# A retention and cosine-gated layer on Trainium2: S, Y and A as quarters of one block with swapped key halves, loads behind the preceding slot's transposes, the first k ahead of the iotas

## The chip, the core and the metric

The kernel runs on one core of one Trainium2 chip. The metric is the device time of one execution in microseconds; 8 runs of the kernel before have a median of 210.26 (210.06 to 210.48). One further execution was taken with the profiler.

## The reference

Two layers follow each other. The first is a retention recurrence with a fixed decay per head; the second is a two-matrix layer gated with a cosine.

```python
B, H, S, D = 4, 8, 768, 64
gamma = 1.0 - 2.0 ** (-5.0 - np.arange(H))
for t in range(S):
    state = gamma * state + k[t] (outer) v[t]        # per batch and head, 64 x 64
    y[t] = D ** -0.5 * q[t] @ state
x = y.transpose(0, 2, 1, 3).reshape(B * S, H * D)    # 3072 x 512
h = x @ w_in                                         # 512 x 2048
out = (h * np.cos(h)) @ w_out                        # 2048 x 512
```

## The kernel before

**Slots.** The sequence is cut into 6 chunks of 128 tokens. A slot `p` is one chunk of two batches (b = 0, 1), 12 slots in all; `ORDER` starts with chunk 0 of both batch pairs and goes through the rest one pair after the other. Within a chunk the recurrence is written as matrix products:

- q and k are loaded (`load`), scaled and cast to bf16 (`conv_q`, `conv_k`; `conv_v` scales v by a decay `gk` that depends on the token's place), and turned so that the head dimension lies in the partitions: by TensorE with `t_mm` and `t_copy` for slots 0 to 5, by a transposing DMA (`dma_t`, on SP) from slot 6 on.
- **A** (`a_mm`): the scores of the chunk's 128 keys against its 128 queries, for 16 pairs of batch and head. DVE multiplies them by a causal mask (`a_mask`, into `am`).
- **Y**: the output of the slot. The first part ("inter", line 428) takes the old state `stb` times q; the second (`intra`, line 414) takes the masked scores times v.
- **S** (`s_mm`, line 460): the state gains k times v, in the PSUM bank `st_ps`; `s_copy` casts it to `stb` for the next slot.

**Quarters.** A and Y work on matrices with 64 rows and 64 columns of weights, and so use the 128x128 array as four quarters: (row half, column half), by `tile_position`. S used two column strips of 128 rows. Where two row halves add into the same PSUM bank, they take turns: `y1_mm` gives one half of the keys to each batch, `hop` is an empty instruction on another engine (SP for slots up to 5, POOL after that) that waits for the end of this first part, and `y2_mm`, which exchanges the halves, waits for it. `intra` leaves out queries 0 to 63 where keys are 64 to 127, since the mask is zero there (64 columns instead of 128); A computed them.

**The block of a slot** in steady state is inter, first part of Y, hop, A of the next slot, second part of Y, S. Around it run the wide matmuls: `f_mm` (x times w_in, four of 512 columns), cosine on ACT (`f_cos`), product on DVE (`f_mul`), and `o_mm` (times w_out), evacuated by ACT (`o_out`) and stored through SP (`o_dma`). Groups of four chunks go through 16 steps `s`, each one `f_mm` of group g and one quarter of an `o_mm` of group g-1; the block of a slot follows step 3 and step 11. The last output tile is split in two halves of 256 columns (`last_o`).

**Order.** Each engine runs its instructions in the order in which they were issued. Up to slot 5 a planner (`Plan`) orders the work with costs, due ranks (`RF`, `RM`, a random addition of `JIT` with seed `SEED`), and counts of free PSUM banks and DMA semaphores; `LOADS` is the order of the loads that POOL issues, `HALF0` says how many of group 0's w_in columns are done slot by slot (`h_mm`). Where the plan has nothing for TensorE early on, `idle_mm` fills with zero matmuls. Past the plan, a hand-written loop issues `block`, `conv` and loads of later slots on SP.

**The start.** POOL makes three iotas, then issues the loads of k, q and k of the slots 0 and 1 (names "K", "Q1", "K1") and v; SP issues the two halves of slot 0's q. DVE makes `dist`, the identity and the mask from the iotas, ACT eight decays `dec` from `dist`, then `gq` and `gk`. Slots 0 and 1 differ: A is a full 128-row product (`a_mm` with `p < 2`), masked with `dec`; one of its tiles is saved by ACT (`a_save`) and masked by POOL (`a_late`) for each slot; `y_first` is the slot's Y, with v as it was loaded (`raw_v`).

Of the kernel before, what the change touches and what calls it, by code (L numbers as in the profile page):

```python
# [162 lines left out]
SEED, JIT, HOLD = 60, 4.0, "PD"  # L163
HALF0, SPARE, RF, RM, COLD = 4, 1, 40.0, 40.0, 5.2
# [3 lines left out]
def kernel(  # L168
# [24 lines left out]
    ORDER = [0, NC] + [x for x in range(1, NP) if x != NC]  # L193
    LATE = NC
# [39 lines left out]
    mask = sb([128, 128], BF16, "mask")  # L234
# [3 lines left out]
    gk = sb([128, NC, H], FP32, "gk")  # L238
# [27 lines left out]
    def load(eng, p, names):  # L266

        bp, c = divmod(ORDER[p], NC)
        for n in names.split():
            t, src = SRC[n[0].lower()]  # L270
            if len(n) == 1:
# [4 lines left out]
                        "b h t d -> t (b h) d"))  # L276
            else:
# [33 lines left out]
    def conv_v(p, b, e):  # L311
        ENG[e].tensor_tensor(out=vb(p)[:, b], in0=vf[p % PRE][:, b],  # L312
                             in1=bc(gk, ORDER[p] % NC), op=ALU.mult)

# [38 lines left out]

    def a_mm(p, u):
        n = p % NB
        bk = held["a", p, u] = [banks.take(), banks.take()]
        ap = [t.rearrange("p (a t) -> p a t", a=HP) for t in bk]
        for a in range(HP):
            h = 4 * u + a
            for x in range(1 if p < 2 else 2):  # L360
                for b in range(2):
                    if p < 2:
                        nc.tensor.matmul(ap[b][:, a, :], lhsT=kt(n, b, h), rhs=qt(n, b, h),
                                         tile_position=(64 * b, 0))
                        continue
                    nc.tensor.matmul(ap[b][ts(x, 64), a, :], lhsT=kt(n, b, h)[:, ts(x, 64)],  # L366
                                     rhs=qt(n, b, h), tile_position=(64 * b, 64 * x),
                                     skip_group_check=True)

    def a_mask(p, b, u):  # L370
        bank = held["a", p, u][b]
        nc.vector.tensor_tensor(  # L372
            out=am[p % 2][b][u], in0=bank.rearrange("p (a t) -> p a t", a=HP),
            in1=(dec[:, b] if p < 2 else mask.unsqueeze(1).to_broadcast([128, HP, 128])),
            op=ALU.mult)
        banks.give(bank)
# [32 lines left out]
    def intra(p, b, a, x, **kw):  # L409

        ms = []
        for j in range(2):
            h = 2 * a + j
            ms.append(nc.tensor.matmul(  # L414
                held["yp", p][b][ts(j, 64), a, 64 * x :], lhsT=vs[p % NB][ts(x, 64), b, h, :],
                rhs=am[p % 2][b][h // 4][ts(x, 64), h % 4, 64 * x :],
                start=False, stop=True, tile_position=(64 * x, 64 * j), skip_group_check=True))
        return ms

    def y1_mm(p):  # L420
# [3 lines left out]
        for a in range(HP):  # L424
            for b in range(2):
                for j in range(2):
                    h = 2 * a + j
                    nc.tensor.matmul(  # L428
                        held["yp", p][b][ts(j, 64), a, :], lhsT=stb[p % 2][ts(b, 64), h, :],
                        rhs=qt(p % NB, b, h), start=(a == 0), stop=False,  # L430
                        tile_position=(64 * b, 64 * j), skip_group_check=True)
        for a in range(HP):
            held["part", p] = intra(p, 1, a, 1) + intra(p, 0, a, 0)

    def hop(p):
        ms = held["part", p]
        held["hop", p] = (nc.sync if p <= 5 else nc.gpsimd).nop(nofuse=True)
        for m in ms:
            after(m, held["hop", p])

    def y2_mm(p):
        for a in range(HP):
            for m in intra(p, 1, a, 0) + intra(p, 0, a, 1):
                if a == 0:
                    after(held["hop", p], m)
# [6 lines left out]

    def has_s(p):
        return p != 1 and (p == LATE or ORDER[p] % NC < NC - 1)

# [75 lines left out]
    def last_o(g, j):  # L531

        o = ob[o_no[0] % 4]
        for hf in range(2):
            bank = banks.take()
            for f in range(KOUT):
                nc.tensor.matmul(bank[:, :256], lhsT=gt[g % 2][:, f, ts(j, 128)],  # L537
                                 rhs=w_out_sb[:, f, ts(hf, 256)],
                                 start=(f == 0), stop=(f == KOUT - 1))
            copy("AD"[hf], o[:, ts(hf, 256)], bank[:, :256])  # L540
            (nc.sync, nc.scalar)[hf].dma_start(
                out=out[ds(o_row(g, j), C), ts(hf, 256)], in_=o[:, ts(hf, 256)])
# [8 lines left out]

    nc.gpsimd.iota(pos, pattern=[[C, NC]], base=1, channel_multiplier=1,
# [5 lines left out]
    load(nc.sync, 0, "q0 q1")  # L558
    load(nc.gpsimd, 0, "K")
# [9 lines left out]
    nc.vector.tensor_scalar(out=mask, in0=dist, scalar1=0.0, scalar2=None, op0=ALU.is_ge)  # L569
# [10 lines left out]
    nc.scalar.activation(out=gk, in_=lgp, func=AF.Exp, scale=-1.0)  # L580
    nc.scalar.activation(out=lnsc, in_=halfpi, func=AF.Sin)
# [9 lines left out]
    HM, HCQ, HCV = "q2", "", ""  # L591
    plan = Plan({"bank": 7, "cos": 3, "sem": 8, "out": 4, "port": 1, "ring": 7}, 6.5)
# [7 lines left out]
    ld["q", 0, 0], ld["q", 0, 1], ld["k", 0, 0], ld["k", 0, 1] = map(at, (3.9, 5.0, 7.4, 7.4))  # L600
# [287 lines left out]
```

## Time and profile before

| what | value |
|---|---|
| median of 8 runs | 210.26 us (210.06 to 210.48) |
| the profiled execution, its own time | 210.43 us |
| its span in the profile | 208.6 us |
| TensorE busy | 201.7 us (97%) |
| ScalarE, VectorE, GpSimd busy | 115.9, 108.0, 80.0 us |
| granted TensorE clock, mean | 0.998 |
| data moved by DMA | 32.05 MB |

PE is TensorE, PEld its weight loads, DVE VectorE, ACT ScalarE, POOL GpSimd, SP SyncE, which only issues DMAs and carries waits here. Times in rows count from the span's start. Matmuls are pipelined: a row's extent holds the tail of its last matmul too, so distances between starts say more than extents. "[0.27 <-POOLq ...]" behind a row is idle time of that engine and what ended it. Some matmul records can be missing, so a count of 14 may stand beside a row of 2.

### The profile page before, as it was taken

The numbers are of one execution on the slowest core, as the hardware profiler recorded it, in microseconds if no ns is written. First come the engines' busy times: TensorE is split into PE (matmuls) and PEld (weight loads), VectorE is DVE, ScalarE is ACT, GpSimd is POOL, SyncE is SP. The second block draws the span as 40 slices with busy tenths as digits, with TensorE's granted clock in tenths as the row PEclk, the third lists the DMA queues.
The fourth block names the chain that finished last, engine by engine and source line by source line (L and its number), as shares of the span: only waits on it lengthen the run. The fifth ranks groups of instructions, "written<-read, shape, count | busy, mean of one in ns | idle before, by whom it ended". The sixth has DMA issues, their size and how long they took to land.

```text
span 208.6 us, 4799 instructions
## 1 busy us (share of the span) xinstructions
PE 201.7 (97%) x1994; PEld 109.2 (52%) x2017; DVE 108.0 (52%) x186; ACT 115.9 (56%) x194; POOL 80.0 (38%) x84
## 2 busy tenths in 40 slices
PE   7999999999999999999999999999999999999993
PEld 2547456789555545445455455454444444444462
DVE  5474888977725647438438438338332334443000
ACT  7677788579655456556556556554545553553120
POOL 8789979999999007007007007000000000000000
PEclk9999999999999999999999999999999999999999
DMA  7999999999999599999894602401101101110222
GB/s 123 185 258 225 309 250 291 209 335 343 343 293 182 148 232 245 229 216 247 201 256 29 176 0 54 150 0 57 50 0 53 50 9 44 50 50 21 80 79 76
DMA packets 57495, 32.05 MB, mean 154 GB/s; under 512 B 46592, under 2 KB 51968, under 8 KB 57472
## 3 DMA queue, kind: packets, MB, share of 16 engines
q0 software_dynamic: 14352, 15.47, 33.6%
q1 hardware_dynamic: 42976, 16.13, 31.8%
q8 instruction: 16, 0.26, 0.5%
q10 hardware_dynamic: 144, 0.13, 0.2%
q14 instruction: 7, 0.06, 0.1%
HBM read 27.26 MB, written 6.29 MB: 161 GB/s over the span
## 4 chain that ended last, share of the span: by engine, by line
PE 91%; DMA 3%; POOL 2%; issue 1%; DVE 1%; POOLq 0%; DVEq 0%
PE bank L517 38%; PE bank L472 31%; PE bank L493 8%; DMA vf<-in_v_dram 3%; PE bank L366 3%; PE bank L414 2%; PE st_ps L460 2%; PE bank L337 2%; PE bank L537 2%; PE bank L428 2%; PE bank L546 1%; POOL ks L273 1%; PE bank L395 1%; POOL qs L273 1%; POOL kx L273 1%
## 5 line engine op out<-in xcount | busy, mean ns | idle before, releaser
L480 ACT ACTIVATE cosb<-bank,halfpi 128x512 bf16<-128x512 f32 x96 | 65.5, 689 | 57.4 <-PE bank L472 46.4
L517 PE MATMUL bank<-w_out_sb,gt 128*128 128x512 bf16 x360 | 90.1, 379 | 0.9 <-issue 0.3
L484 DVE TENSOR_TENSOR gt<-bank,cosb 128x512 bf16<-128x512 f32 x76 | 51.6, 688 | 55.3 <-ACT cosb L480 55.3
L472 PE MATMUL bank<-xt,w_in_sb 128*128 128x512 bf16 x289 | 74.8, 379 | 0.8 <-issue 0.3
L517 PEld LDWEIGHTS <-gt 128*128 128x128 bf16 x368 | 35.7, 98 | 42.3
L472 PEld LDWEIGHTS <-w_in_sb 128*128 128x128 bf16 x304 | 28.9, 98 | 34.0 <-DMA w_in_sb<-in_moe_w_in_dram 0.2
L308 POOL TENSOR_TENSOR qs<-qf,gq 128x512 bf16<-128x512 f32 x18 | 18.5, 1044 | 44.9 <-PE bank L414 44.8
L372 DVE TENSOR_TENSOR am<-bank,mask 128x512 bf16<-128x512 f32 x40 | 24.8, 679 | 0.3 <-PE bank L366 0.3
L312 POOL TENSOR_TENSOR vs<-vf,gk 128x512 bf16<-128x512 f32 x22 | 22.7, 1044 | 1.5 <-DMA vf<-in_v_dram 1.2
L297 ACT COPY ob<-bank 128x512 f32<-128x512 f32 (+1 forms) x24 | 13.8, 576 | 15.5 <-PE bank L517 13.9
L493 PE MATMUL bank<-xt,w_in_sb 128*128 128x256 bf16 x160 | 18.8, 273 | 0.0
L297 ACT CAST xt<-bank 128x512 bf16<-128x512 f32 x24 | 12.9, 589 | 9.7 <-PE bank L414 9.0
L501 DVE TENSOR_TENSOR gt<-bank,cosb 128x512 bf16<-128x512 f32 x20 | 13.5, 688 | 8.8 <-ACT cosb L480 8.8
L493 PEld LDWEIGHTS <-w_in_sb 128*128 128x128 bf16 x160 | 15.4, 98 | 2.7
L299 DVE CAST stb<-st_ps 128x512 bf16<-128x512 f32 x10 | 6.9, 689 | 11.1 <-PE st_ps L460 11.1
L546 PE MATMUL bank<-zero 128*128 128x512 bf16 x33 | 10.8, 455 | 1.1 <-DVE halfpi L562 1.1
L297 ACT CAST ks<-kf 128x512 bf16<-128x512 f32 x20 | 11.5, 629 | 0.0
L273 POOL DMA_DIRECT2D vf<-in_v_dram x8 | 9.5, 1194 | 0.0
L297 ACT COPY qkt<-bank 128x512 bf16<-128x512 bf16 x13 | 7.1, 594 | 2.8 <-PE bank L337 2.5
L414 PE MATMUL bank<-am,vs 64*64 64x64 bf16 (+1 forms) x320 | 8.3, 205 | 0.1
L299 DVE COPY ob<-bank 128x256 f32<-128x256 f32 x1 | 0.4, 425 | 13.4 <-PE bank L537 13.4
L366 PE MATMUL bank<-qkt 64*64 64x128 bf16 x320 | 7.2, 218 | 0.0
(59 smaller groups left out, 109.7 us busy)
## 6 DMA issues: line engine op xcount, KB each, us to landing
out_dram<-ob SPq DMA_DIRECT2D x23, 256.0 KB, 2.3
vf<-in_v_dram POOLq DMA_DIRECT2D x8, 512.0 KB, 8.5
qf<-in_q_dram POOLq DMA_DIRECT2D x6, 512.0 KB, 10.3
kf<-in_k_dram POOLq DMA_DIRECT2D x6, 512.0 KB, 9.8
w_out_sb<-in_moe_w_out_dram POOLq DMA_DIRECT2D x4, 512.0 KB, 12.5
qf<-in_q_dram SPq DMA_DIRECT2D x4, 512.0 KB, 4.4
kf<-in_k_dram SPq DMA_DIRECT2D x4, 512.0 KB, 6.2
vf<-in_v_dram SPq DMA_DIRECT2D x4, 512.0 KB, 6.6
```

Of the source, the lines that this page charges most:

```text
L273: eng.dma_start(out=t.rearrange("p b h d -> p (b h) d"), in_=src[ds(2 * bp, 2), :, ds(c * C, C), :].rearrange("b h t d -> t (b h) d"))
L297: nc.scalar.copy(out=out, in_=in_)
L308: ENG[e].tensor_tensor(out=qb(p)[:, b], in0=qf[p % PRE][:, b], in1=bc(gq, ORDER[p] % NC), op=ALU.mult)
L312: ENG[e].tensor_tensor(out=vb(p)[:, b], in0=vf[p % PRE][:, b], in1=bc(gk, ORDER[p] % NC), op=ALU.mult)
L366: nc.tensor.matmul(ap[b][ts(x, 64), a, :], lhsT=kt(n, b, h)[:, ts(x, 64)], rhs=qt(n, b, h), tile_position=(64 * b, 64 * x), skip_group_che ...
L372: nc.vector.tensor_tensor(out=am[p % 2][b][u], in0=bank.rearrange("p (a t) -> p a t", a=HP), in1=(dec[:, b] if p < 2 else mask.unsqueeze(1 ...
L472: nc.tensor.matmul(bank, lhsT=w_in_sb[:, i, ts(f, 128)], rhs=xt[g % 2][:, i, :], start=(i == 0), stop=(i == KIN - 1))
L480: nc.scalar.activation(out=cb, in_=bank, func=AF.Sin, bias=halfpi)
L484: nc.vector.tensor_tensor(out=gt[g % 2][:, f, :], in0=bank, in1=cb, op=ALU.mult)
L493: nc.tensor.matmul(bank[:, ts(e, 256)], lhsT=w_in_sb[:, i, ts(f + e, 128)], rhs=xt[g % 2][:, i, ts(hf, 256)], start=(i == 0 and e == 0), s ...
L501: nc.vector.tensor_tensor(out=gt[g % 2][:, f : f + 2, ts(hf, 256)], in0=bank.rearrange("p (f t) -> p f t", f=2), in1=cb.rearrange("p (f t) ...
L517: nc.tensor.matmul(bank, lhsT=gt[g % 2][:, f, ts(j, 128)], rhs=w_out_sb[:, f, :], start=(f == 0), stop=(f == KOUT - 1))
```

## The change

- **One block in quarters** (`y_block`). S is split into two row halves of 64 keys, so that it too uses quarters: 32 matmuls instead of 16, in two parts with a hop between them. Inter, Y, S and the A of the next slot are listed per row half and put in an order by `quarters`, which always takes the matmul whose quarter is free first; second parts are held back for 250 ns after the first by its reckoning. Hops go to SP for slots up to 4, to POOL after that.
- **A leaves out its dead quarter**: 64 columns where keys are all later than the queries. From slot 8 on (`SWAP`) the two halves of the keys are exchanged for half of the heads, by loads in pieces ("ks", "vs": six DMAs each), so that the dead quarter falls on different row and column halves. There are a second mask and a table `gk3` with exchanged halves, filled by three small DMAs on SP.
- **Loads past the plan**: slot p+3 instead of p+4, issued behind the transposes of p+2; v's behind the next output store. The output store of a step now stands ahead of the transposes.
- **Start**: k of slot 0 is issued before the iotas; the second half of slot 0's q on ACT's queue.
- **End**: the last output tile is split 384 and 128.
- **Plan**: no random addition, `HALF0` 6 instead of 4, other due ranks, a few loads in another place, other costs for the blocks.

```diff
-SEED, JIT, HOLD = 60, 4.0, "PD"
-HALF0, SPARE, RF, RM, COLD = 4, 1, 40.0, 40.0, 5.2
+SEED, JIT, HOLD = 0, 0.0, "PD"
+HALF0, SPARE, RF, RM, COLD = 6, 1, 50.0, 30.0, 5.2
...
+            elif n[1] == "s":
+                fl = t[p % PRE].rearrange("p b h d -> p (b h) d")
+                for x in range(2):
+                    for lo, n4, th in ((0, 4, x), (4, 8, 1 - x), (12, 4, x)):
+                        eng.dma_start(
+                            out=fl[ts(x, 64), ds(lo, n4), :],
+                            in_=src[ds(2 * bp, 2), :, ds(c * C + 64 * th, 64), :]
+                            .rearrange("b h t d -> t (b h) d")[:, ds(lo, n4), :])
...
+    def second(p, x, b, u):
+        return x ^ (u ^ b if p >= SWAP else 0)
+    def a_one(p, ap, u, a, b, x):
+        h, lo = 4 * u + a, 64 * second(p, x, b, u)
+        return nc.tensor.matmul(
+            ap[b][ts(x, 64), a, lo:], lhsT=kt(p % NB, b, h)[:, ts(x, 64)],
+            rhs=qt(p % NB, b, h)[:, lo:], tile_position=(64 * b, 64 * x), skip_group_check=True)
...
+    def quarters(rows):
+        free = [[0.0, 0.0], [0.0, 0.0]]
+        left = [list(r) for r in rows]
+        while left[0] or left[1]:
+            best = None
+            for r in range(2):
+                for c in range(2):
+                    nxt = next((m for m in left[r] if m[0] == c), None)
+                    if nxt:
+                        t = max(free[r][c], nxt[2])
+                        if best is None or t < best[0]:
+                            best = (t, r, nxt)
+            t, r, m = best
+            left[r].remove(m)
+            free[r][m[0]] = t + m[1] / 2.4
+            m[3]()
+    def hop_on(p):
+        return nc.sync if p <= 4 else nc.gpsimd
...
+    def s_part(p, r):
+        x = 1 if p == LATE else p
...
+                    m = nc.tensor.matmul(
+                        st_ps[ts(b, 64), h, :], lhsT=kb(x)[ts(r, 64), b, h, :],
+                        rhs=vb(x)[ts(r, 64), b, h, :],
+                        start=(ORDER[x] % NC == 0 and h == 0 and r == 0), stop=True,
+                        tile_position=(64 * r, 64 * b), skip_group_check=True)
...
+    def told(what, p, part, m):
+        key = (what, p)
+        if part == 0:
+            held.setdefault(("ms", key), []).append(m)
+            if len(held["ms", key]) == (32 if what == "y" else 16):
+                w = held["hop", key] = hop_on(p).nop(nofuse=True)
+                for x in held.pop(("ms", key)):
+                    after(x, w)
+        elif held.get(("first", key), 0) < 4:
+            held["first", key] = held.get(("first", key), 0) + 1
+            after(held["hop", key], m)
...
+    def y_block(p, a_next):
...
+        t1 = sum(m[1] for m in y_inter(p, 0) + y_part(p, 0, 0)) / 4.8 + 250
+        t2 = sum(m[1] for m in y_inter(p, 0) + y_part(p, 0, 0) + s_part(p, 0)) / 4.8 + 250
+        for r in range(2):
+            ms = y_inter(p, r) + y_part(p, r, 0)
+            if has_s(p) and r == 0:
+                ms += s_part(p, 0)
+            if a_next:
+                ms += a_rows(p + 1, r)
+            ms += late(y_part(p, r, 1), t1)
+            if has_s(p) and r == 1:
+                ms += late(s_part(p, 1), t2)
+            rows.append(ms)
+        return quarters(rows)
...
-        for hf in range(2):
+        for i, (lo, n) in enumerate(((0, 384), (384, 128))):
...
+    load(nc.gpsimd, 0, "K")
+    load(nc.sync, 0, "q0")
+    load(nc.scalar, 0, "q1")
     nc.gpsimd.iota(pos, pattern=[[C, NC]], base=1, channel_multiplier=1,
...
-    load(nc.sync, 0, "q0 q1")
-    load(nc.gpsimd, 0, "K")
...
+    for x in range(2):
+        nc.vector.tensor_scalar(out=mask[1][ts(x, 64), :], in0=dist[ts(x, 64), :],
+                                scalar1=(64.0, -64.0)[x], scalar2=None, op0=ALU.is_ge)
...
+    for x in range(2):
+        nc.sync.dma_start(out=gk3[ts(x, 64), ds(n, n)], in_=gk3[ts(1 - x, 64), :n])
+    nc.sync.dma_start(out=gk3[:, ds(2 * n, n)], in_=gk3[:, :n])
...
-    HM, HCQ, HCV = "q2", "", ""
+    HM, HCQ, HCV = "k2", "", "o2"
...
-    for p in (PL + 2, PL + 3):
-        load(nc.sync, p, "q k v")
+    load(nc.sync, PL + 2, "q ks vs")
...
             if p < NP and r == 3:
                 block(p)
-                if p + 2 < NP:
-                    conv(p + 2)
-                if p + 4 < NP:
-                    load(nc.sync, p + 4, "q k v")
             if s % 4 == 3:
                 o_dma(g - 1, s // 4)
+            if p + 2 < NP and r == 3:
+                conv(p + 2)
+            if p + 3 < NP and s % 4 == 3:
+                load(nc.sync, p + 3, "q ks" if r == 3 else "vs")
```

## The prediction

> **What bounds the kernel now.** I read the page's busy times and its chain first.
>
> ```profile
> PE 201.7 (97%) x1994; PEld 109.2 (52%) x2017; DVE 108.0 (52%) x186; ACT 115.9 (56%) x194; POOL 80.0 (38%) x84
> ...
> PE 91%; DMA 3%; POOL 2%; issue 1%; DVE 1%; POOLq 0%; DVEq 0%
> ```
>
> TensorE is busy for 97% of the span and is 91% of the chain, so an edit counts only where it shortens PE's stream or PE's early waits. Next the timeline of PE, for the block of slot 9 and, with the weight loads, for the last block (slot 11):
>
> ```profile
> 92.15 1.03 PE L517 MATMUL bank<-w_out_sb,gt 128*128 128x512 bf16 x4
> 93.11 0.42 PE L428 MATMUL bank<-qkt,stb 64*64 64x128 bf16 x16
> 93.36 0.33 PE L414 MATMUL bank<-am,vs 64*64 64x128 bf16 x14
> 93.49 0.22 PE L366 MATMUL bank<-qkt 64*64 64x128 bf16 x2
> 93.52 0.22 PE L414 MATMUL bank<-am,vs 64*64 64x128 bf16 x2
> 93.55 0.69 PE L366 MATMUL bank<-qkt 64*64 64x128 bf16 x30
> 94.03 0.42 PE L414 MATMUL bank<-am,vs 64*64 64x128 bf16 x16
> 94.38 0.44 PE L460 MATMUL st_ps<-vs,ks 128*64 128x64 bf16 x16
> 94.76 1.04 PE L472 MATMUL bank<-xt,w_in_sb 128*128 128x512 bf16 x3
> ```
> ```profile
> 155.56 0.28 PEld L414 LDWEIGHTS <-vs 64*64 64x64 bf16 x16
> ...
> 156.11 0.25 PEld L414 LDWEIGHTS <-vs 64*64 64x64 bf16 x16 [0.27 <-POOLq L437]
> ```
>
> The columns are start, extent, engine, line, operation, shape and count; a quarter is a 64x64 corner of the array, four of which can work at once. The order is inter (L428), Y part 1 (L414), A (L366), Y part 2, S (L460). The wide stream would have gone on at 92.15+4x0.216=93.015, so the block costs 0.095 (drain in) + 94.76-93.11=1.65, in all 1.745 us; the same on slots 4 to 6 is 1.69, 1.715, 1.745, on slot 3 (no A) 1.375, on slot 11 (no A, no S) 1.19. Prices: sixteen transposes of 128 columns take 0.89 us in the chain, 55.6 ns each; S loads weights every 14.7 ns ((0.33-0.11)/15 in its row of loads) in two column strips, so 64 columns take 29 ns. The busiest quarter holds 4 inter, 4 Y, 8 A, 4 Y of 128 columns, 20x55.6=1.11, and then S 8x29=0.23: 1.34 of the 1.65. The rest is mostly drain: Y part 2 runs 0.35 for 0.22 of work before S may start, S 0.38 for 0.23 before the wide stream. In the last block the second half's loads start 0.38 after the last of the first half (155.56+0.28-0.11=155.73): that is a hop over POOL, with nothing to cover it.
>
> Last, the start, by engine:
>
> ```profile
> 0.84 0.15 POOL L552 IOTA pos<- 128x6 f32 x1 [0.39 <-POOLq L872]
> ...
> 1.42 1.37 POOL L273 DMA_DIRECT2D ks<-in_k_dram  x1 [0.25 <-issue]
> ...
> 11.29 1.54 POOL L284 DMA_DIRECT2D w_in_sb<-in_moe_w_in_dram  x2
> 13.56 1.27 POOL L384 TENSOR_TENSOR am<-gt 128x512 bf16<-128x512 f32 x1 [0.72 <-ACT gt L380]
> ```
> ```profile
> 2.39 2.44 ACT L577 ACTIVATE gt<-gt,lnsc 128x128 f32<-128x128 f32 x8 [0.37 <-DVE gt L572]
> ...
> 6.61 0.57 ACT L297 COPY qkt<-bank 128x512 bf16<-128x512 bf16 x1
> ```
> ```profile
> 15.32 0.64 PE L395 MATMUL bank<-am,gt 128*64 128x128 bf16 x16
> ```
>
> ACT's first copy waits for nothing but ACT itself, which waited for `dist`, which waited for the iotas.
>
> **Blocks.** S becomes 32 matmuls of 64 rows, in the same four quarters as A and Y: one block of 112 instead of 96, no drain inside. A and Y leave out the dead quarter, but where keys aren't swapped (slots below 8) it falls always on the same quarters. Fullest quarter, slots 4 to 6: 4+8+8 of 128 columns and 8 of 64, 1.11+0.23=1.34; slot 7 (A of slot 8 is swapped): four of the A drop to 64, 1.24; slots 8 to 10: 4 inter, 4+4 Y, 4+4 A, 8 S = 12x55.6+16x29=1.13. Around it lie 0.095 in and 0.13 to 0.15 out, together 0.23. Added: a second hop, for S (each 0.38, covered by about 0.30 of other quarters' work by the order's spacing), so 0.06 to 0.12 a block. I take 1.40, 1.30 and 1.25 inside: 1.63, 1.53, 1.48. Against before: slots 4 to 6 -0.06-0.085-0.115=-0.26; slot 7 -0.21; slots 8 to 10 3x-0.265=-0.80. Slots 2 and 3 have no A to lie behind S's hop: inter, Y, S 0.22+0.22+0.23, then 0.38, then S 0.23 = 1.28, so 1.5 against 1.375: +0.11 on slot 3, 0 on slot 2, where part of the time was a wait. Slot 11: Y of 12 by 0.17 twice, -0.04. Sum -1.20. Floor: no loss at all, -1.9. Ceiling: the pace at which weight-and-matmul pairs enter. The nearest rows are the 14 of L414 (loads every 9.2 ns, (0.23-0.11)/13), the A of slot 4 (13.7, (0.48-0.11)/27) and of slot 9 (16.2, (0.69-0.22)/29 above). At 9.2 the 112 take 1.03 and bind nowhere; at 13.7, 1.53; at 16.2, 1.81, a block of 2.04. I take the first, since A's pace is explained by its full quarters (four in 55.6 ns is 13.9); the others make a rival.
>
> [...] In the rows A's two lone matmuls (93.49) start before Y's last two (93.52), which precede them in the program: the two row halves of the array run past each other, so that short and long matmuls need not hold each other up. [...]
> Thirty A start in 0.47 us, one in 16 ns. [...]
>
> **Start.** K's issue (1.37) goes ahead of the iotas on POOL: they end at 2.54 to 2.8 instead of 1.17, while Q1, K1 and v0 are issued when they were. DVE makes `dist` 1.37 to 1.63 later, plus two half masks at 0.14 each; so ACT's exponentials, table load and first copy move by 1.65 to 1.9, 6.61 to 8.3. K lands 0.6 earlier, which helps nothing behind that copy. Following rows: second k transposes at 8.9, DVE's copy to 9.8 (8.80 before), A's second half 9.85, ACT's saved bank 10.3 to 10.9, POOL's late mask to 12.2, two w loads 1.54, and now also q2's issue (1.2) ahead of the second late mask: 14.95 to 16.2, where it ended at 14.83. Slot 1's first Y needs that mask: 16.27 instead of 15.32, +0.95. One filler (0.21) after it is gone. I take +0.70; bounds +0.2 (DMA sets the start instead) and +1.2 (the iotas pay 0.25 more).
>
> **Tail.** The last evacuation (205.10, 0.42 for 256 columns; the copy of 512 is 0.69) halves to 0.29: -0.13, bounds 0 and -0.25.
>
> **At nothing.** q1's issue on ACT (0.5) lies in ACT's wait for `dist`. The three copies of gk follow ACT at about 7 on SP, whose next deed is slot 2's hop, after 31.5. Swapped loads are 13 issues a slot on SP: by 0.39 (least row) 5.1, plus transposes 2.6 and outputs 0.7, in a slot of 15.57; they have a whole slot until they are read. They wait behind the transposes, which wait for POOL's q casts (2.1); output stores now stand before these. If a piece cost over 0.85 SP would be the bound. Hops on POOL from slot 5: its casts take 4.2 of each slot, ending 11 before the next block; only on slot 5 is the cover thin (POOL ended 68.02, the hop comes at 68.45), 1 us if it is gone. The planned order up to 70 us holds the same matmuls, with o loads ahead of k3: counts by prices make 53.4 of the 53.95 us from 15.89 to slot 5's end, so little can be won: 0, from -0.3 to +0.5.
>
> **Sum.** -1.20+0.70-0.13=-0.63 on the profiled execution's 210.43 (span 208.6 and 1.83 around it): 209.80. That run is 0.17 above the median of 210.26, so 209.6 for the median.
>
> **Rivals.**
> - *Pairs enter too slowly* (slower). At 13.7 ns, 112 pairs take 1.53 and a block 1.76: slots 4 to 10 lose 0.22, slot 3 0.11, the start 0.70, and 0.17 comes back: 211.1. It decides from about 12.5 ns on, where the blocks save less than the start costs. For: A's pace in late blocks, and no row shows a faster pace past 30 pairs. Against: those rows are bound by quarters. 0.25.
> - *The start hides it* (faster): K's earlier landing and the fillers (7, 1.61 us) absorb the shift: 208.9. For: those fillers are idle time. Against: their end and the late mask lie in the same line. 0.17.
> - *The new planned order or the late loads stall PE* by 1 us once: 210.6. 0.12.
> - *The blocks save only half*, 0.6: start and blocks cancel: 210.2, nothing to tell. 0.11.
>
> **How the numbers follow.** The forecast has 0.35; its own range, from its bounds, is 208.9 to 210.2. A difference of 0.2% (0.42 us) is about what can be told here. Faster: forecast 0.30, hidden start 0.17, stall 0.03, together 0.50. Same: forecast 0.05, slow entry 0.03, stall 0.04, half 0.08, together 0.20. Slower: slow entry 0.22, stall 0.05, half 0.03, together 0.30. The range reaches from 208.6, short of both gains at once, to 211.3, past the slow entry at 13.7 ns.
>
> **What would show it.** Right: slots 8 to 10 take about 1.5 us between wide matmuls, slots 4 to 6 about 1.6; S lies among A and Y in the same quarters, with no drain ahead of it; ACT's first copy at about 8.3 and slot 1's first Y at about 16.3. Wrong: pairs evenly 14 ns apart; a PE wait on the hop over 0.1; slot 1's first Y at 15.3; a wait of POOL or ACT on the swapped pieces.

## The result, and the profile after

The changed kernel takes 211.34 us (median of 11 runs, 211.05 to 212.38) beside 210.28 for the kernel before (31 runs): a ratio of 1.0060, with a 95% interval of 1.0048 to 1.0072. It is slower by 0.6%; 209.6 had been forecast. The profiled execution took 211.69, with a span of 209.9 against 208.6.

The busy line and the chain come first:

```profile
PE 200.8 (96%) x2143; PEld 109.2 (52%) x2167; DVE 110.6 (53%) x188; ACT 115.8 (55%) x194; POOL 80.0 (38%) x84
...
PE 86%; DVE 3%; ACT 3%; POOL 3%; issue 2%; POOLq 0%; DVEq 0%
```

TensorE is busy for 0.9 us less, as the blocks were meant to bring about, but its share of the chain falls from 91% to 86%: DVE, ACT and POOL now hold 9% of it. Time has been added where TensorE waits for them.

Next the timeline of TensorE for the block of slot 8 (the first with swapped keys), in the columns used above. L490 is inter, L476 Y, L385 A, L504 S, L586 and L631 the wide matmuls:

```profile
110.49 1.03 PE L631 MATMUL bank<-w_out_sb,gt 128*128 128x512 bf16 x4
111.45 0.42 PE L490 MATMUL bank<-qkt,stb 64*64 64x128 bf16 x16
111.69 0.34 PE L476 MATMUL bank<-am,vs 64*64 64x128 bf16 x16
111.87 0.20 PE L504 MATMUL st_ps<-vs,ks 64*64 64x64 bf16 x2
111.87 0.22 PE L385 MATMUL bank<-qkt 64*64 64x64 bf16 x2
...
112.63 0.23 PE L504 MATMUL st_ps<-vs,ks 64*64 64x64 bf16 x3
112.79 1.04 PE L586 MATMUL bank<-xt,w_in_sb 128*128 128x512 bf16 x3
```

S and A start together at 111.87, without the drain that lay ahead of S before. The wide stream would have gone on at 110.49+4x0.216=111.355, so the block costs 112.79-111.355=1.435 us, where it cost 1.745 before. The last of its pairs start at about 112.65, so 112 pairs enter in 1.2 us, one every 11 ns.

The start, in the timelines of POOL, DVE, ACT and TensorE:

```profile
1.26 1.31 POOL L277 DMA_DIRECT2D ks<-in_k_dram  x1 [0.81 <-POOLq L973]
...
2.85 0.16 POOL L673 IOTA gt<- 128x16 f32 x1
2.94 1.17 POOL L277 DMA_DIRECT2D qs<-in_q_dram  x1
4.11 1.15 POOL L277 DMA_DIRECT2D kx<-in_k_dram  x1
...
16.09 1.20 POOL L277 DMA_DIRECT2D qf<-in_q_dram  x1
17.27 1.31 POOL L416 TENSOR_TENSOR am<-gt 128x512 bf16<-128x512 f32 x1
```
```profile
3.04 0.29 DVE L679 TENSOR_TENSOR gt<-gt 128x128 f32<-128x128 f32 x1 [2.02 <-POOL gt L673]
3.37 0.80 DVE L683 TENSOR_SCALAR ident<-gt 128x128 bf16<-128x128 f32 x1
3.51 0.72 DVE L684 TENSOR_SCALAR mask<-gt 128x128 bf16<-128x128 f32 x1
4.15 1.15 DVE L686 TENSOR_SCALAR mask<-gt 64x128 bf16<-64x128 f32 x2
...
17.30 1.58 DVE L311 CAST gt<-vf 128x512 bf16<-128x512 f32 x1
```
```profile
5.91 2.45 ACT L695 ACTIVATE gt<-gt,lnsc 128x128 f32<-128x128 f32 x8 [3.38 <-DVE gt L690]
...
10.13 0.57 ACT L309 COPY qkt<-bank 128x512 bf16<-128x512 bf16 x1
```
```profile
18.30 1.04 PE L427 MATMUL bank<-am,gt 128*64 128x128 bf16 x16
19.28 0.94 PE L607 MATMUL bank<-xt,w_in_sb 128*128 128x256 bf16 x7
```

Follow the ends. The identity ends at 4.17, just behind POOL's issue of Q1 (2.94+1.17=4.11). The two half masks end at 5.30, just behind that of K1 (4.11+1.15=5.26). The raw cast of v at 17.30 ends at 18.88, 0.3 behind POOL's late mask (18.58). In the kernel before the identity took 0.23 and that cast 0.41:

```profile
1.53 0.23 DVE L568 TENSOR_SCALAR ident<-gt 128x128 bf16<-128x128 f32 x1
...
2.06 0.29 DVE L572 TENSOR_TENSOR gt<-gt 128x128 f32<-128x128 f32 x1
...
14.79 0.41 DVE L299 CAST gt<-vf 128x512 bf16<-128x512 f32 x1
```

ACT's exponentials begin at 5.91 (2.39 before), its first copy is at 10.13 (6.61), slot 1's first Y at 18.30 (15.32), and the first h matmul at 19.28 (15.89).

Set against the kernel before by the starts of four rows, the span divides like this:

| stretch | before | after | difference |
|---|---|---|---|
| span's start to the first h matmul | 15.89 | 19.28 | +3.39 |
| from there to slot 6's block | 61.66 | 61.19 | -0.47 |
| slot 6's block to the first wide matmul behind slot 11's | 78.90 | 77.78 | -1.12 |
| from there to the last output row | 44.91 | 44.90 | -0.01 |
| last output row to the end | 7.24 | 6.75 | -0.49 |

The sum is +1.30, the difference of the spans. From slot 6 on the blocks give about what they should (-1.165 by the forecast), and the start takes three times as much.

### The profile page after: what moved, and what is told of

Its sections match the earlier page's. It is cut to its first block, busy times and chain, and to the rows that moved or that the text cites. A ratio compares the mean times of both kernels' runs of the same rounds, so it can differ in the third digit from the quotient of the medians.

```text
span 209.9 us, 5182 instructions
## 1 busy us (share of the span) xinstructions
PE 200.8 (96%) x2143; PEld 109.2 (52%) x2167; DVE 110.6 (53%) x188; ACT 115.8 (55%) x194; POOL 80.0 (38%) x84
## 4 chain that ended last, share of the span: by engine, by line
PE 86%; DVE 3%; ACT 3%; POOL 3%; issue 2%; POOLq 0%; DVEq 0%
PE bank L631 38%; PE bank L586 28%; PE bank L607 9%; PE bank L476 2%; PE bank L385 2%; PE bank L651 2%; PE bank L357 2%; PE bank L490 1%; PE st_ps L504 1%; POOL am L416 1%; ACT gt L695 1%; DVE am L404 1%; POOL w_in_sb L296 1%; POOL ks L277 1%; ACT L703 1%
## 5 line engine op out<-in xcount | busy, mean ns | idle before, releaser
L631 PE MATMUL bank<-w_out_sb,gt 128*128 128x512 bf16 x359 | 89.9, 379 | 1.1 <-issue 0.5
L586 PE MATMUL bank<-xt,w_in_sb 128*128 128x512 bf16 x281 | 73.0, 379 | 0.6 <-issue 0.2
L631 PEld LDWEIGHTS <-gt 128*128 128x128 bf16 x368 | 35.5, 98 | 42.2
L586 PEld LDWEIGHTS <-w_in_sb 128*128 128x128 bf16 x296 | 28.3, 98 | 33.1
L607 PE MATMUL bank<-xt,w_in_sb 128*128 128x256 bf16 x176 | 20.4, 273 | 0.0
L607 PEld LDWEIGHTS <-w_in_sb 128*128 128x128 bf16 x176 | 17.0, 98 | 2.7
L311 DVE CAST stb<-st_ps 128x512 bf16<-128x512 f32 x9 | 6.2, 690 | 11.5 <-PE st_ps L504 9.5
L476 PE MATMUL bank<-am,vs 64*64 64x128 bf16 (+1 forms) x320 | 10.2, 206 | 0.2
L385 PE MATMUL bank<-qkt 64*64 64x64 bf16 (+1 forms) x320 | 8.3, 207 | 0.0
L311 DVE COPY qkt<-bank 128x512 bf16<-128x512 bf16 x12 | 4.7, 417 | 5.8 <-PE bank L357 5.8
```

Source lines behind the costliest of these rows:

```text
L385: return nc.tensor.matmul(ap[b][ts(x, 64), a, lo:], lhsT=kt(p % NB, b, h)[:, ts(x, 64)], rhs=qt(p % NB, b, h)[:, lo:], tile_position=(64 * ...
L476: m = nc.tensor.matmul(held["yp", p][b][ts(j, 64), a, lo:], lhsT=vs[p % NB][ts(r, 64), b, h, :], rhs=am[p % 2][b][h // 4][ts(r, 64), h % 4 ...
L586: nc.tensor.matmul(bank, lhsT=w_in_sb[:, i, ts(f, 128)], rhs=xt[g % 2][:, i, :], start=(i == 0), stop=(i == KIN - 1))
L607: nc.tensor.matmul(bank[:, ts(e, 256)], lhsT=w_in_sb[:, i, ts(f + e, 128)], rhs=xt[g % 2][:, i, ts(hf, 256)], start=(i == 0 and e == 0), s ...
L631: nc.tensor.matmul(bank, lhsT=gt[g % 2][:, f, ts(j, 128)], rhs=w_out_sb[:, f, :], start=(f == 0), stop=(f == KOUT - 1))
```

## Experiments

The kernels differ from the changed one unless another is named. All medians stand against the kernel before on the same chip (210.28 to 210.36).

### The issue of k: undone, and alone

`e1_iotas_first` puts the iotas ahead of k's issue again:

```diff
-    load(nc.gpsimd, 0, "K")
     load(nc.sync, 0, "q0")
     load(nc.scalar, 0, "q1")
     ... iotas
+    load(nc.gpsimd, 0, "K")
```

> The changed kernel with the iotas back ahead of k's issue on POOL; all else as changed. Theory (the start costs it all): in the changed kernel slot 1's first Y moved from 15.32 to 18.30; here the iotas end near 1.2, ACT's first copy comes at about 6.9 (two half masks more), slot 1's first Y at 15.4 to 15.8, and 2.5 to 2.9 us come back: 208.4 to 208.9, faster than the kernel before. Rival (the new planned order and the late loads cost it): slot 1's first Y moves, but the lead is lost again before slot 6, and the time stays within 0.5 of 211.3.

Measured: 209.75, ratio 0.9965 (0.9948 to 0.9982). One edit turns the change from a loss into a small gain, but 208.4 to 208.9 had been expected, and only its shortest execution is there. In the profile, which is of this one (208.88), slot 1's first Y is at 15.33, but it takes 1.10 instead of 0.64, and the half masks take 1.00 beside k's issue.

`e2_before_k_first` is the kernel before with only this edit, the other way round:

```diff
+    load(nc.gpsimd, 0, "K")
     ... iotas
     load(nc.sync, 0, "q0 q1")
-    load(nc.gpsimd, 0, "K")
```

> The kernel before with k's issue put ahead of the iotas and nothing else. Theory: identity and mask on DVE (0.23 each) are held until POOL's issue of Q1 ends, ACT's first copy moves from 6.6 to about 9.5, and most of it arrives at the end: 212.4 to 213.0, plus 2.1 to 2.7. Rival (only the plain shift of the iotas, 1.4 to 1.6, as predicted): plus 0.9 to 1.3, 211.2 to 211.6, DVE's rows at 0.23 as before. Second rival (the start is hidden): within 0.4 of 210.3.

Measured: 212.05, ratio 1.0072 (1.0051 to 1.0093): +1.71. The identity takes 0.80 there too, ACT's exponentials begin at 4.72 and slot 1's first Y is at 17.06, 1.74 later. That is less than the 2.1 to 2.7 expected, but the issue moved alone costs more than twice what the forecast gave to the whole start.

### What holds DVE

`e4_q1_issue_waits` makes POOL wait with Q1's issue until DVE has made the masks and `dist`:

```diff
-    nc.vector.tensor_scalar(out=far, in0=dist, ...)
+    last = nc.vector.tensor_scalar(out=far, in0=dist, ...)
     nc.vector.tensor_tensor(out=dist, in0=dist, in1=far, op=ALU.max)
+    after(last, nc.gpsimd.nop(nofuse=True))
     ... then Q1, K1 and v as before
```

> The changed kernel with an empty instruction on POOL between the iotas and the issue of Q1, which waits for DVE's masks: so POOL issues nothing while DVE makes identity and masks. Theory (DVE waits for POOL's DMA issue): identity and mask last 0.23 each instead of 0.80 and 0.72, the two half masks under 0.4 together instead of 1.15, ACT starts at 4.5 to 4.7 instead of 5.91, though Q1, K1 and v land about 1.2 later; time 209.8 to 211.0. Rival (the operations are slow for another reason, such as their operands): they last as long as in the changed kernel and the time grows by about 1.

Its DVE and POOL timelines:

```profile
3.38 0.23 DVE L683 TENSOR_SCALAR ident<-gt 128x128 bf16<-128x128 f32 x1
3.52 0.22 DVE L684 TENSOR_SCALAR mask<-gt 128x128 bf16<-128x128 f32 x1
3.65 0.45 DVE L686 TENSOR_SCALAR mask<-gt 64x128 bf16<-64x128 f32 x2
```
```profile
4.90 1.78 POOL L277 DMA_DIRECT2D qs<-in_q_dram  x1 [1.88 <-DVE gt L690]
```

Identity and mask begin at the same time as in the changed kernel, and with POOL quiet they take 0.23 and 0.22, the half masks 0.45. So it was POOL's issue that held them. It seems to work the other way too: Q1's issue, now beside DVE's casts of q, takes 1.78 instead of 1.17. What the two engines share, and so why one holds the other, no run shows. Nor is every instruction held: beside the same issue of k (1.42 to 2.79) the tensor-tensor at 2.06 keeps its 0.29 in the kernel before, and the half masks of e1 (1.81, 1.00) are held to the issue's end. When an issue begins to hold differs: in the kernel before, a tensor-scalar instruction that begins 0.39 behind the start of k's issue still takes 0.22; in the changed kernel the second half mask, which begins 0.26 behind that of K1's (at 4.37), takes 0.94. No run here shows what sets this point.

The time stays at 211.32 (ratio 1.0039, 1.0025 to 1.0052), where 209.8 to 211.0 had been expected. The first h matmul is 1.23 earlier than in the changed kernel, yet slot 6's block is only 0.19 earlier. Most of the lead is lost where TensorE's transposes wait for POOL's cast of q, a wait that the changed kernel doesn't have:

```profile
51.96 0.40 PE L357 MATMUL bank<-ident,qs 128*128 128x128 bf16 x4 [0.62 <-POOL qs L320]
```

All of POOL's loads and casts have moved back, so POOL's issues cannot simply be made to wait.

`e3_dist_ahead_of_masks` has DVE make `dist` first, in the buffer `far`, and the masks after it:

```diff
+    nc.vector.tensor_scalar(out=far, in0=dist, scalar1=0.0, scalar2=1.0e6, ...)
+    nc.vector.tensor_tensor(out=far, in0=dist, in1=far, op=ALU.max)
     ... identity, mask, half masks
-    nc.vector.tensor_scalar(out=far, in0=dist, scalar1=0.0, scalar2=1.0e6, ...)
-    nc.vector.tensor_tensor(out=dist, in0=dist, in1=far, op=ALU.max)
     ... exponentials, now with in_=far
```

> The changed kernel with DVE's order in the start changed: the decay distances that ACT waits for first (written to the other buffer), identity and masks behind them. Theory (DVE's one-input operations wait for the end of the DMA issue that POOL is in): the first of them still lasts 0.8, ACT starts at 4.4 to 4.6 instead of 5.91, its first copy comes at 8.7 to 8.9, and 0.8 to 1.3 us come back: 210.0 to 210.5. Rival (the delay is only the iotas'): ACT gains the three masks' 0.5 at most, 210.8 to 211.3.

Measured: 212.99 (1.0121, 1.0103 to 1.0140), a miss. ACT's exponentials began at 5.87, no earlier. ACT's table load, otherwise done at 2.5, itself waited until 4.58, for DVE; why it did so was not traced. The edit did not do what it was made for, and says little about the rest.

### The half masks

`f3_half_masks_later` keeps k first and makes the half masks only after the raw cast of slot 1's second v; TensorE's order is that of the changed kernel:

```diff
-    for x in range(2): nc.vector.tensor_scalar(out=mask[1][ts(x, 64), :], ...)
-    nc.vector.tensor_tensor(out=dist, in0=dist, in1=far, op=ALU.max)
+    nc.vector.tensor_tensor(out=distm, in0=dist, in1=far, op=ALU.max)
...  in raw_v
+        if (p, b) == (1, 1):
+            ... the two half masks, from dist
```

> The changed kernel, with k's issue still first; only the two half masks are made later, behind the raw cast of slot 1's second v, from a copy of the distances that is kept. TensorE's instructions and their order are those of after. Theory (two prices in the start: 1.7 us for k's issue, 1.2 us for the half masks that DVE runs beside POOL's issue of K1): ACT's exponentials begin at about 4.7 instead of 5.91, slot 1's first Y at 17.1 instead of 18.30, time 210.1 us (209.8 to 210.5). Rival: the late mask on POOL and the raw cast beside it set slot 1's first Y, whatever ACT does before: 211.3.

```profile
4.72 2.45 ACT L697 ACTIVATE gt<-gt,lnsc 128x128 f32<-128x128 f32 x8 [2.19 <-DVE gt L692]
```
```profile
17.32 1.04 PE L432 MATMUL bank<-am,gt 128*64 128x128 bf16 x16
18.30 1.92 PE L612 MATMUL bank<-xt,w_in_sb 128*128 128x256 bf16 x16
```

Measured: 210.31 (ratio 1.0000, 0.9987 to 1.0013), 1.03 less than the changed kernel; exponentials 1.19 earlier, slot 1's first Y 0.98. The half masks cost a full microsecond, where the forecast gave them 0.28. Its exponentials begin at 4.72, as in e2; beside e2 the first Y takes 1.04 instead of 0.64, as DVE's raw cast of v (16.32, 1.57) again ends 0.3 behind POOL's late mask (17.60), where in e2 that cast takes 0.41.

### Both out of the way, and a surprise of the planner

`g1_quiet_start` joins the two (iotas first, half masks later), and also sets the planner's `HM` from "k2" back to "q2": `HM` names the load whose issue is put behind POOL's two late masks:

```diff
-    HM, HCQ, HCV = "k2", "", "o2"
+    HM, HCQ, HCV = "q2", "", "o2"
```

> The run with the iotas first, and besides: the two half masks made after slot 1's raw v instead of ahead of the decay distances, and q2's issue behind POOL's late mask again. Theory (what was left of the start's loss were DVE operations held by POOL): the half masks in the chain took 1.00 us and DVE's raw v beside the late mask 1.66; here ACT starts at 2.4 instead of 3.41, DVE's raw v lasts 0.4 to 0.7, slot 1's first Y ends near 15.9 instead of 16.4, and 0.4 to 0.8 us come back: 208.9 to 209.4. Rival (the start's rest is fixed by v's landing and the fillers): within 0.2 of the run with the iotas first.

Measured: 215.25 (1.0235, 1.0210 to 1.0260), a miss by over 5 us. The start did work: slot 1's first Y is at 15.25 and takes 0.64, the first h matmul is at 15.82. But slot 6's block begins at 84.10 instead of 80.47. With one setting changed, the planner had written another order, and TensorE's rows show where it loses:

```profile
60.79 7.07 PE L636 MATMUL bank<-w_out_sb,gt 128*128 128x512 bf16 x32
...
72.45 0.33 PE L481 MATMUL bank<-am,vs 64*64 64x64 bf16 x6 [0.94 <-DVE am L409]
...
75.27 1.86 PE L591 MATMUL bank<-xt,w_in_sb 128*128 128x512 bf16 x4 [0.67 <-ACT xt L310]
```

Here 32 wide matmuls stand ahead of slot 4's block, and none between it and slot 5's. Slot 5's block then waits 1.5 us for DVE's masks and 0.7 for ACT, the wide matmuls behind it another 0.7. From 73 to 79 us the granted clock reads 0.50, and the four wide matmuls at 75.27 enter every 0.42 us instead of 0.216: part of the loss is TensorE at half speed behind these waits. `f4_quiet_start_same_order` has the same start with "k2" kept.

> As g1_quiet_start (iotas first, half masks later), but with the planner's setting for slot 2 kept as in after, so that TensorE's order is that of after and of e1_iotas_first. Theory (the order that the planner made for g1 cost its 5.5 us, at k3's load and slot 5): 209.4 to 209.8 us, as e1_iotas_first (209.75) or up to 0.4 below, slot 6's block at about 77.3 to 77.7. Rival (the later half masks themselves disturb the planned part): 214 to 215 us.

Measured: 210.12 (0.9975, 0.9957 to 0.9992), with slot 6's block at 78.98. Its eight wide matmuls at 60.99 and 24 at 64.31 stand around slot 4's block, and its granted clock reads 1.00 there. The 5 us are therefore the order's. But 210.12 lies 0.3 above what was expected, and the ten runs spread from 208.78 to 210.27; the profiled execution, 210.21, shows why. TensorE's first rows in it:

```profile
1.06 3.17 PE L665 MATMUL bank<-zero 128*128 128x512 bf16 x7 [1.06 <-DVE halfpi L682]
5.39 0.61 PE L362 MATMUL bank<-ident,qs 128*128 128x128 bf16 x4 [1.16 <-DVE qs L312]
5.79 1.06 PE L665 MATMUL bank<-zero 128*128 128x512 bf16 x2
6.64 0.63 PE L362 MATMUL bank<-ident,qs 128*128 128x128 bf16 x4
7.07 2.34 PE L665 MATMUL bank<-zero 128*128 128x512 bf16 x5
```

The fillers take 0.44 us each where they usually take 0.22, until 9.4 and behind a gap of 1.16. e1, with the same gap (1.17), has its two fillers in 0.59 and its five in 1.24. So the same instructions run at half speed in one profiled execution and at full speed in another; that f4's other runs divide in the same way is read from their times alone. The gap has the cause already met: q's first cast, which begins at 4.25 instead of 3.77, takes 1.08 beside K1's issue.

### The gap filled

`m1_gap_filled` is f4 with ten fillers instead of seven ahead of the first transposes; `m2_after_gap_filled` is the changed kernel with thirteen.

```diff
-    for i in range(7):
+    for i in range(10):     # m2: 13
         idle_mm("E", 2)
```

> f4_quiet_start_same_order with ten instead of seven fillers ahead of the first transposes, so that TensorE has no gap from 4.2 to 5.4 us. Theory (TensorE's speed in the start is what splits the runs): fillers at 0.22 from about 5.4 on, slot 1's first Y at about 15.3 to 15.6 in every run, 208.7 to 209.1 us and no second group. Rival (something else splits them, such as the loads' landing): the two groups stay, median 210.1.

> The changed kernel with thirteen instead of seven fillers ahead of the first transposes, which covers its gap from 4.2 to 6.9 us. Theory (ACT's late exponentials set its start, TensorE's speed hardly counts): 210.9 to 211.4 us, first copy of ACT still at 10.1, slot 1's first Y at 17.9 to 18.3. Rival (the slow TensorE is a good part of the start's loss): 210.3 or less. Without the group at 212.3 that the changed kernel has.

m1: 209.66 (0.9961, 0.9947 to 0.9975), and its eight runs lie between 209.16 and 209.90, where six of f4's ten lie above 210.1. Filling the gap ends this upper group; the lowest times (208.78 and 209.02 in f4) are gone as well. In m1's profile TensorE is still at half speed behind the fillers, but for a shorter time than in f4's, where it lasts until 9.4:

```profile
1.06 4.45 PE L665 MATMUL bank<-zero 128*128 128x512 bf16 x10 [1.06 <-DVE halfpi L682]
...
5.80 1.06 PE L665 MATMUL bank<-zero 128*128 128x512 bf16 x2
...
6.93 1.24 PE L665 MATMUL bank<-zero 128*128 128x512 bf16 x5
```

What sets the end of the half speed no run shows. The granted clock reads 1.00 from 6 to 9.5 us in f4's profile and has a mean of 1.00 in m1's, and does not show it.

But 208.7 to 209.1 was not reached. The reason is a third place of the kind already met, in m1's DVE and POOL timelines:

```profile
14.71 2.40 DVE L312 CAST gt<-vf 128x512 bf16<-128x512 f32 x1
```
```profile
14.46 1.28 POOL L421 TENSOR_TENSOR am<-gt 128x512 bf16<-128x512 f32 x1
15.68 1.20 POOL L278 DMA_DIRECT2D kf<-in_k_dram  x1
```

The raw cast of v meets the late mask and then k2's issue, and ends at 17.11, 0.23 behind the second of them, instead of after 0.41; half of slot 1's first Y waits for it until 17.16.

m2: 211.22 (1.0044, 1.0030 to 1.0057), as expected. ACT's first copy is still at 10.13. The gap of 2.68 in the changed kernel is thus not what makes its median. None of m2's five runs lies at 212.3, where three of the changed kernel's eleven lie; five are few to say that this group is gone. The changed kernel's own profile has TensorE at half speed behind that gap, and here the granted clock does show it: 0.77 from 7 to 9.5 us and 0.55 from 9.5 to 12. The same five fillers, in the changed kernel and in m2:

```profile
8.13 2.11 PE L660 MATMUL bank<-zero 128*128 128x512 bf16 x5
```
```profile
8.13 1.24 PE L660 MATMUL bank<-zero 128*128 128x512 bf16 x5
```

The first h matmul is at 18.80 in m2, 0.48 earlier than in the changed kernel. The +3.39 above stays all the same, for the profile of the kernel before has some of it too: t1 (below), with the same start and its two fillers at 4.68 in 0.59 instead of 1.06, has its first h matmul at 15.42, and 18.80-15.42 is 3.38.

### Blocks and tail alone

`g2_blocks_alone` is the kernel before with the new blocks (quarters, swap, loads, hops), but with its own start, planner's settings, load list and tail; the half masks are made late. Against the changed kernel:

```diff
-SEED, JIT, HOLD = 0, 0.0, "PD"
-HALF0, SPARE, RF, RM, COLD = 6, 1, 50.0, 30.0, 5.2
+SEED, JIT, HOLD = 60, 4.0, "PD"
+HALF0, SPARE, RF, RM, COLD = 4, 1, 40.0, 40.0, 5.2
...  iotas first, q1 on SP, half masks behind raw_v(1, 1), tail 256 and 256
-    HM, HCQ, HCV = "k2", "", "o2"
+    HM, HCQ, HCV = "q2", "", ""
...  LOADS as in the kernel before
```

> The kernel before with the blocks alone: quarters, swapped halves from slot 8, loads of p+3 behind the transposes, hops as changed; start, plan settings, loads and the 256/256 tail as before, half masks after slot 1's raw v. Theory (blocks win what the trace of the changed kernel shows): slots 8 to 10 take 1.43 instead of 1.745, slot 7 1.63, slot 6 1.69, slot 11 1.12; in all 1.1 to 1.3 less, 209.0 to 209.3. Rival (the blocks' gain is eaten by the late loads or by slots 2 to 5): 209.9 to 210.4.

Measured: 209.07 (0.9938, 0.9923 to 0.9952), 1.27 less than before. From slot 6's block to slot 11's its periods are 15.43, 15.35, 15.31, 15.31 and 15.26, where every one was 15.56.

`g3_no_swap` is g1 with unswapped keys and whole loads, `g4_old_tail` is g1 with the tail in 256 and 256:

```diff
-    SWAP = 8
+    SWAP = NP
...
-                load(nc.sync, p + 3, "q ks" if r == 3 else "vs")
+                load(nc.sync, p + 3, "q k" if r == 3 else "v")
...  and in g4_old_tail alone
-        for i, (lo, n) in enumerate(((0, 384), (384, 128))):
+        for i, (lo, n) in enumerate(((0, 256), (256, 256))):
```

> The quiet start without the swap of key halves (and so with whole loads of k and v on SP): quarters, one block, dead quarter left out. Theory (the fullest quarter sets a block): all blocks from slot 6 on take 1.69 as slot 6 does, so 0.06 more on slot 7, 0.26 on slots 8 to 10, 0.07 on slot 11: 0.8 to 1.0 more than with the swap. Rival (what won is the drain that is gone): within 0.2 of the quiet start.

> The quiet start with the last tile in halves of 256 as before. By the prediction's term 0.13 is lost; by the traces (from the first of the last tile's matmuls to the end 7.24 before, 6.75 changed) 0.5. Rival: none can be told, within 0.1.

Measured: 216.28 and 216.09, so +1.03 and +0.84 on g1. Neither difference is wholly the part taken out. The mean granted clock is 0.982 to 0.984 in all runs of both, in g1 in four of six (the other two have 0.992); against these four (215.10 to 216.18) the differences are about 0.7 and 0.5. In g3 slot 6's block, which no swap touches, is already 0.54 later; from slot 7's block to slot 11's it takes 61.74 against 61.41 in g1: the swap is worth 0.33 in four blocks here, or 0.08 each. Unswapped, every period is 15.43 or 15.44. In g4 slot 6's block is 0.82 later, and the tail itself takes 6.93 instead of 6.73.

`t1_tail_alone` is the kernel before with only the tail in 384 and 128, `f1_blocks_and_tail` is g2 with it.

```diff
-        for hf in range(2):
+        for i, (lo, n) in enumerate(((0, 384), (384, 128))):
```

> The kernel before with only the new tail, 384 and 128 columns. By the forecast's term -0.13 (bounds 0 and -0.25): 210.15 us, ratio 0.9994. By after's trace, whose end behind the last row's first matmul is 0.49 shorter: 209.8, ratio 0.9977. Rival: the end of the span is set by ACT's copy of 384 and its store, longer than that of 256: 210.4.

> The kernel g2_blocks_alone (start, planned order and load list of before, new blocks) with the new tail: last output row in 384 and 128 columns instead of 256 and 256. If the tail is worth what the forecast gave it (0.13), 208.9 us, ratio to the kernel before about 0.993; if it is worth the 0.49 by which the end of after's trace is shorter, 208.6. If the new blocks and the tail pay at all without the new start, it is faster than both kernels. Rival: the uneven halves only trade places and it stays at 209.1.

```profile
204.80 0.29 DVE L299 COPY ob<-bank 128x128 f32<-128x128 f32 x1 [13.36 <-PE bank L537]
```

t1: 210.11 (0.9995, 0.9985 to 1.0005): 0.17 less by the medians, which the interval does not tell from nothing; the last copy takes 0.29 instead of 0.42, the 0.13 of the forecast.

f1: **208.78** (0.9926, 0.9913 to 0.9939). It beats both kernels: the new blocks and tail on the old start and order. (Its profiled execution, 210.30, is the slowest of its seven; it has the half-speed fillers of f4.)

Along one chain the medians read: f1 208.78; with the new planned order, q1 on ACT and more fillers (m1) 209.66; with k's issue first (f3, seven fillers) 210.31; with the half masks in the start (the changed kernel) 211.34. No run divides the 0.88 between f1 and m1.

## Why the prediction was wrong, point by point

- **Blocks: right.** -1.20 was forecast, -1.27 measured alone (g2). Slot by slot g2's periods give -0.13, -0.21, -0.25, -0.25 and -0.30 for slots 6 to 10, where -0.115, -0.21 and three times -0.265 were forecast. That the totals agree so well is partly luck: in g2's trace slot 6's block begins 0.20 later than before, and the end of the span is shorter by about as much, which no term of the blocks foresaw. In the changed kernel's trace slots 6 to 11 gave -1.12 where the terms make -1.165; slot 8 cost 1.435, not 1.48; slot 11 gave about what was said. The swap brought less in g1 (0.08 a block) and more in the changed kernel (its periods fall from 15.52 on slot 6 to 15.26 from slot 8 on) than the forecast 0.15. The prediction named the block it showed slot 9's; starting at 93.11 it is slot 7's. Since all of these cost 1.745, no number moves.
- **Start: the step that failed.** The term was +0.70, bounds +0.2 and +1.2; the trace has +3.39 at the first h matmul, and 0.47 less than that at slot 6's block. In medians, k's issue moved alone cost 1.71 (e2) and the half masks in the start 1.03 (f3), 2.74 together; with the blocks' -1.27 and the tail's -0.17 that makes +1.30, beside +1.06 measured. Three sizes in the term were wrong. The forecast moved ACT's exponentials by 1.65 to 1.9, and they moved by 3.52: DVE's first instruction 1.84 later, the identity and mask 0.50 longer, and the half masks 1.17 instead of the forecast 0.28. The 1.84 exceeds the forecast's 1.37 to 1.63 by 0.2 to 0.5 and is the iotas' (e4 has it with POOL quiet). The 0.50 and the 0.89 beyond the half masks' 0.28 are one mistake: DVE's instructions were priced as they stood in the trace of before, though the edit moved them beside POOL's issues of Q1 and K1. The first copy was to be at 8.3 and was at 10.13. Then "q2's issue ahead of the second late mask" was rightly seen (its end 16.2 by the forecast, 18.58 measured), but not that the raw cast of v beside it is held as well, which makes the first Y take 1.04 and the first h matmul another 0.4 later.
- **The warning was in the trace of before.** Its casts of q and of v took 0.43 and 0.41 once, and 0.69 and 0.71 at 4.66 and 12.37; the slow ones lie across the end of a POOL issue (K1's at 5.09, that of w at 12.83) and end 0.25 behind it:

```profile
3.77 0.43 DVE L299 CAST qs<-qf 128x512 bf16<-128x512 f32 x1 [0.83 <-DMA qf<-in_q_dram]
4.66 0.69 DVE L299 CAST qs<-qf 128x512 bf16<-128x512 f32 x1 [0.46 <-DMA qf<-in_q_dram]
```

- **Tail: right in size, as far as can be told.** -0.13 forecast, -0.17 alone (t1), its bounds held, though the interval reaches zero. The -0.49 of the comparison of traces is not all the tail's: t1 shows 7.05 for the same stretch against 7.24, and kernels with the new blocks and the old tail show 6.97 (g2) and 6.93 (g4). What the blocks' edits do there was not traced to a cause.
- **Planned order: not settled.** 0 was taken, from -0.3 to +0.5; from the first h matmul to slot 6's block the trace has -0.47, of which the blocks of slots 3 to 5 explain -0.035 by the forecast. It may only give back part of the late start: by the medians of f1 and m1 the new order, together with q1 on ACT and the fillers, costs 0.88. How thin an order is, g1 showed: one setting, and a loss of 5 us.
- **At nothing: held where it was said, with one exception.** SP waits for outputs (70.2 us on ACT's copies), not on its 13 pieces a slot, and no TensorE wait on a hop stands in the blocks shown. Not seen was that the first half of q comes later when q1 goes out beside it on ACT (its cast begins at 4.25 instead of 3.77 in f4) and is then cast beside K1's issue: TensorE's gap of 1.16, and with it the half speed of some runs.
- **The rivals.** "Pairs enter too slowly" gave 211.1, next to the time measured, and is false: the pairs enter every 11 ns and the blocks pay. That its number was met is luck. "The start hides it" is refuted by e2. A stall of the planned order did not occur in the changed kernel. "Blocks save only half" is refuted by g2.

## What to carry to other kernels

When an edit moves an instruction of DVE in time, price it by what POOL does at its new place, not by its row in the old trace (the identity took 0.23 there and 0.80 in the new one); and where one form has two durations in a trace (here q's casts, 0.43 and 0.69), find out what stood beside the longer one before using the shorter. Keep small mask work out of the window in which POOL issues the first loads, unless something waits for it: the half masks there cost 1.03 (f3). Change the streams of a loop and the order of a start separately: here the loop's gain (1.27, g2) was real and a start edit that moved 1.3 us of POOL work ahead of three iotas cost more than all of it (1.71, e2).

## What the runs showed of the hardware that had not been expected

- A POOL DMA issue held casts and tensor-scalar instructions of DVE to its end: the identity takes 0.23 in e4 and 0.80 in the changed kernel, the two half masks 0.45 and 1.15, q's first cast 0.43 in the kernel before and 1.08 in f4. A cast of v beside POOL's own tensor instruction goes from 0.41 (kernel before) to 1.58 (changed kernel), and one beside a tensor instruction and the issue behind it to 2.40 (m1). It seems to go both ways: Q1's issue, 1.17 in the changed kernel, takes 1.78 beside DVE's casts in e4.
- Not from its first moment: in the kernel before, three tensor-scalar instructions between 1.53 and 2.03 ran at 0.22 to 0.23 beside k's issue (from 1.42), while in e1 the half masks that begin at 1.81 end with it, at 2.81.
- Behind a gap of 1.16 that begins at 4.2 us, TensorE ran the same stream at half speed in f4's profile (fillers 0.44), and behind one of 1.17 at full speed in e1's (0.22). The times fit this: f4's ten lie between 208.78 and 210.27, and f1's profiled execution, with half-speed fillers, took 210.30 beside 208.35 to 208.92 of its other six. With fillers over the gap (m1) the half speed ended by 6.9 us in the one profile taken, and the upper group of times was gone in eight runs.
- The granted clock of the profile did not show the half speed of f4 (1.00 with fillers at 0.44), but did show a fall back to it later (0.55 in the changed kernel's profile, 0.50 in g1's).
- 112 pairs of weights and matmul in four quarters enter at 11 ns each over 1.2 us (slot 8 of the changed kernel). The kernel before had 9.2 ns over 14 pairs, 13.7 over 28 and 16.2 over 30.
